# A recurrence chain next to an expert layer: running two neighbouring items half an item apart

## The chip, the cores and the metric

One core of a Trainium2 chip runs the whole program. The metric is the device time of one execution in microseconds (us), lower is better: 1274.45 us is the median of 3 runs of the kernel before (1274.09 to 1287.01).

## The reference, cut

Three layers follow each other. The first is a linear recurrence over 768 steps for 4 x 8 heads, each with a 40 x 40 state:

```python
for t in range(S):
    y[:, :, t] = np.einsum('bhd,bhde->bhe', rt, state)
    Sa = np.einsum('bhde,bhe->bhd', state, at)
    state_decay = state * wt[:, :, None, :] - np.einsum('bhd,bhe->bhde', Sa, bt)
    state = state_decay + np.einsum('bhd,bhe->bhde', vt, kt)
```

Its output goes through a dense layer (`h = x @ w_in`, `g = max(0.01*h, h)`, `g @ w_out`, 3072 tokens of 320, hidden 2048), and that through eight experts with top-1 routing (`relu(x @ w1[e]) @ w2[e]`, scaled by the gate).

## The kernel before, in words

Time is cut into chunks of 64 steps, and the recurrence within a chunk is solved with matrix products. An **item** is one chunk for eight heads; there are 48. Items alternate between two states, `S[0]` for even and `S[1]` for odd numbers, so item i needs the state that item i-2 left and nothing of item i-1. The Tile scheduler sets the order on each engine from the order of the code and priorities; every engine then works in that order and holds at an instruction whose input is not there.

For the work on an item i this text uses one letter for each group of TensorE matmuls, with the lines of the kernel before:

- **T** (L551): four transposes of loaded columns; DVE multiplies them to `KB` (L553).
- **P** (L559, L564): the two masked products; ACT copies them out (L570), POOL masks them (L572).
- **S** (L591): state times right sides, into the PSUM tile `y`; ACT copies (L595).
- **R** (L601): right-hand sides of the triangular system; ACT copies to `X` (L602).
- **V** (L607): inverse times right-hand sides; DVE (L612) and ACT (L614) write the result, with its sign turned, into `F`.
- **z** (L622): the state's update, which DVE adds to the state (L624). **y** (L628): the outputs; DVE scales them to `Y` (L631) and SP stores them (L636).
- Items 6, 7, 14, 15, 30, 31, 38 and 39 also turn the state back (L643).

T and P of item i+1 belong to the generator `late(i+1)`, which is stepped beside `chain(i)`: T before S of item i, P right behind V of item i. The loads for item j (`late_load(j)`, L530 to L540, all issued by SP) stand in the code behind item j-3.

Two other streams fill TensorE between these groups. `moe` is the dense layer: L686 (first product, 8 matmuls of 256 columns a piece) and L707 (second product, 6 of 328 columns a piece). `early` prepares the triangular inverses for eight items at a time: products on L463, a long run of DVE work (L475 to L501), and two small products for each of four chunks (L507, L515). `run` mixes the streams with `merge`, which takes steps in proportion to given weights: per item five steps of the chain, ten of `early` and eight of `moe`.

PSUM banks are handed out by `s.banks`: bank 0 to `early`, bank 1 to T and P (`sl`), bank 2 to `y` (`cy`), bank 3 to R, V, z and the turns (`cx`), 4 to 7 to `moe`. So one bank holds `y` of every item from 4 on.

Behind item 47 the rest of `moe` runs, and then the experts (phase 2, L1073 to L1146), which the change leaves alone.

Of the kernel before, what the change touches and what calls it, by code (L numbers as in the profile page):

```python
# [16 lines left out]
ALU = mybir.AluOpType  # L17
# [7 lines left out]
RST = 4  # L25
NFC = FF // 128
# [7 lines left out]
HC = 75  # L34
FB = 7
HI = 5
# [13 lines left out]
P0 = 5  # L50
P1 = 5
# [4 lines left out]
def bc(ap, shape):  # L56
    return ap.to_broadcast(shape)
# [73 lines left out]
class Phase1:  # L131
    def __init__(s, tc, es, I, out, x1d, chip):
        s.tc, s.nc, s.es, s.I, s.out, s.x1d, s.chip, s.lg = tc, tc.nc, es, I, out, x1d, chip, chip.lg
        nc = s.nc
        g = nc.gpsimd
        s.ident = chip.ident
        bank = lambda *k: Ring([chip.bank[n] for n in k])
        s.banks = {"se": bank(0), "sl": bank(1), "cy": bank(2), "cx": bank(3), "m1": bank(4, 5), "m2": bank(6, 7),
                   "cy1": bank(6), "cx1": bank(7)}
        s.dp = es.enter_context(tc.tile_pool(name="dp", bufs=1, space=DRAM))  # L140
        s.right = chip.room("p1", "right")
        A = s.right.new
# [34 lines left out]
        for h in range(2):  # L177
            m = s.nmask[64 * h:64 * h + 64, :]
# [71 lines left out]
    def decide(s):  # L250
        nc, v = s.nc, s.nc.vector
        v.reduce_max(s.lim[:, 0:1], s.chip.flags, axis=mybir.AxisListType.X)
        pt = s.psum("se")[0:1, 0:128]
# [164 lines left out]

    def early(s, e):
        nc = s.nc  # L420
        ps = lambda: s.psum("m1") if e == 0 else s.psum("se")
# [4 lines left out]
        for c4 in range(4):  # L426
# [33 lines left out]
            for p in range(8):  # L460
                for pi in range(2):
                    q = 64 * (1 - pi)
# [79 lines left out]
    def late(s, i):  # L542
# [4 lines left out]
        la = lL[:, 512:1024].rearrange("q (k p t) -> q k p t", k=2, t=64)  # L547
        nc.sync.dma_start(W[q104], s.dW[i // 2][:, p4])
        pw = s.psum("sl")
# [4 lines left out]
        yield  # L554
        ps = s.psum("sl").rearrange("q (p t) -> q p t", t=128)
# [10 lines left out]
        yield  # L566
        for pi in range(2):
            r = 64 * pi
            Fv = F[r:r + 64, :, pi, 0:128]
            nc.scalar.copy(Fv, ps[r:r + 64])  # L570
            Fv = Fv.rearrange("q p (a t) -> q p a t", a=2)
            nc.gpsimd.affine_select(out=Fv, in_=Fv, compare_op=ALU.is_gt, fill=0.0, base=0,  # L572
                                    pattern=[[0, 4], [0, 2], [1, 64]], channel_multiplier=-1)
        yield


    def chain(s, i, beside=iter(())):
        nc = s.nc
        hh, C, gg = i // 24, (i // 2) % 12, i % 2
        F, RI, W, KB = s.slot(i)  # L580
        S, X, Y = s.S[gg], s.X[i % 2], s.Y[i % 2]
        e = hh * 3 + C // 4
        Inv = s.Inv[e % 2][:, C % 4, 4 * gg:4 * gg + 4]
        v = lambda t: t[:, 0:416].rearrange("q (p t) -> q p t", t=104)
        if C == 0 and hh == 1:
            nc.vector.memset(S, 0.0)
        cy, cx = ("cy", "cx") if i > 3 or i % 2 == 0 else ("cy1", "cx1")
        y = v(s.psum(cy))
        for p in range(4):
            for q in (64, 0):  # L590
                nc.tensor.matmul(y[q:q + 40, p, :], lhsT=S[q:q + 40, p, :], rhs=RI[q:q + 40, p, :],  # L591
                                 start=(p == 0), stop=False, skip_group_check=True)
        for pi in range(2):
            q = 64 * (1 - pi)
            nc.scalar.copy(F[q:q + 40, :, pi, 64:168], y[q:q + 40])  # L595
        yield
        x = v(s.psum(cx))
# [4 lines left out]
        nc.scalar.copy(X, x)  # L602
        yield
        x = v(s.psum(cx))
# [10 lines left out]
        for _ in beside:  # L615
            pass
        yield
        z = s.psum(cx)[:, 0:160].rearrange("q (p t) -> q p t", t=40)
        for p in range(4):
            for pi in range(2):  # L620
                q = 64 * (1 - pi)
                nc.tensor.matmul(z[q:q + 40, p, :], lhsT=F[:, p, pi, 128:168], rhs=KB[:, p, 1 - pi, :], start=True, stop=True)  # L622
        for q in (64, 0):
            nc.vector.tensor_tensor(S[q:q + 40], S[q:q + 40], z[q:q + 40], op=ALU.add)  # L624
        for p in range(4):
            for pi in range(2):
                q = 64 * (1 - pi)
                nc.tensor.matmul(y[q:q + 40, p, 0:64], lhsT=KB[:, p, 1 - pi, :], rhs=F[:, p, pi, 64:128],  # L628
                                 start=False, stop=True, skip_group_check=True)
# [8 lines left out]
        if C % RST == RST - 1 and C < 11:  # L638
            def turn(x):
                t = s.psum("cx")[:, 0:160].rearrange("q (p t) -> q p t", t=40)  # L640
                for p in range(4):
                    for q in (64, 0):
                        nc.tensor.matmul(t[q:q + 40, p, :], lhsT=x[q:q + 40, p, :], rhs=s.ident[q:q + 40, q:q + 40],  # L643
                                         start=True, stop=True)
                return t
            t = turn(S)
            for q in (64, 0):
                nc.vector.tensor_tensor(s.ST[q:q + 40], t[q:q + 40], bc(W[q:q + 40, :, 64:65], [40, 4, 40]), op=ALU.mult)
            t = turn(s.ST)
            for q in (64, 0):  # L650
                nc.scalar.copy(S[q:q + 40], t[q:q + 40])
            yield


    def moe_load(s, v):
# [74 lines left out]
    def run(s, p2):  # L730
# [68 lines left out]
        for i in range(48):  # L799
# [21 lines left out]
            next(beside, None)  # L821
# [615 lines left out]
```

## Time and profile before

| | |
|---|---|
| median of 3 runs | 1274.45 us |
| profiled execution, its own time | 1275.27 us |
| span of that execution (first to last instruction) | 1273.6 us |
| mean granted TensorE clock | 0.942 |
| PE (TensorE matmuls) busy | 1037.1 us, 81% |
| DVE busy | 800.0 us, 63% |
| ACT busy | 511.8 us, 40% |
| POOL busy | 408.0 us, 32% |

PE is the engine that is busiest, yet busy shares are a mean over very different stages; what counts is which wait ends last in a stage. "Granted clock" is the share of full speed that TensorE was given; it takes the values 1.0 (2.4 GHz) and 0.5 (1.2 GHz), and a mean between them says how the time was divided.

How the rows further down read. A stretch: its bounds and length in us, then busy us and number of instructions of PE, PEld (weight loads), DVE, ACT and POOL, the granted clock, the DMA share and GB/s. A timeline: start, duration, engine (SPq is SP's queue), line, operation, output<-inputs, shapes, count, and in brackets the idle time before it and what ended it; instructions of a line that follow each other are merged. Waits: who waited for whom, us in total, times, the longest. Groups by line: busy us, mean ns of one, idle time before them and what ended it.

### The profile page before, as it was taken

Reading aid. Unit: us, or ns where it says so; the run is one execution under the profiler, and the core shown is the slowest. Engines: PE = TensorE matmul, PEld = TensorE weight load, DVE = VectorE, ACT = ScalarE, POOL = GpSimd, SP = SyncE. Lnnn points to the kernel's source line nnn. Section 1 sums busy time; section 2 is a strip of 40 time slices with the busy share of each in tenths; the row PEclk is TensorE's granted clock in tenths of the full one; section 3 lists DMA queues with packets and bytes.
Section 4 is the critical chain, followed back from the end, with each engine's and each line's share of the span. In section 5 each row is a group of like instructions: output and inputs, shape, how many; then the busy total and the mean of one; then the engine's idle time right before and its main releaser. Section 6 shows DMA issues by size and latency. Waiting matters only on the chain. (4 is left out here: it accounts for less than half of the span.)

```text
span 1273.6 us, 31259 instructions
## 1 busy us (share of the span) xinstructions
PE 1037.1 (81%) x12429; PEld 937.0 (74%) x12429; DVE 800.0 (63%) x1677; ACT 511.8 (40%) x1113; POOL 408.0 (32%) x458
## 2 busy tenths in 40 slices
PE   1348943599889989898979988999998968979994
PEld 1336732478778878787878878889898958878983
DVE  4698597894696558855884579544368445543541
ACT  1334442345435354455434543444443235332330
POOL 3364453444321332234222332122242321432210
PEclk9999999999998989998987989999999988989998
DMA  6665265347534654466434644233233444533100
GB/s 166 155 169 138 76 170 153 110 100 181 147 93 101 151 148 104 108 163 162 104 102 105 166 118 113 71 96 91 73 110 103 132 125 126 183 104 106 32 21 20
DMA packets 215735, 149.52 MB, mean 117 GB/s; under 512 B 152820, under 2 KB 195979, under 8 KB 213061
## 3 DMA queue, kind: packets, MB, share of 16 engines
q1 hardware_dynamic: 211949, 138.47, 41.7%
q0 software_dynamic: 3504, 7.75, 2.0%
q8 instruction: 122, 2.00, 0.7%
q14 instruction: 160, 1.31, 0.4%
HBM read 112.39 MB, written 37.21 MB: 117 GB/s over the span
## 5 line engine op out<-in xcount | busy, mean ns | idle before, releaser
L707 PE MATMUL bank<-w,m 128*128 128x328 f32 x792 | 151.2, 329 | 1.6 <-ACT m L691 1.3
L1123 PE MATMUL bank<-p,p 128*128 128x256 f32 (+1 forms) x704 | 121.5, 332 | 33.3 <-issue 26.9
L1123 PEld LDWEIGHTS bank<-p,p 128*128 128x128 f32 x704 | 113.8, 208 | 37.8 <-issue 30.0
L686 PE MATMUL bank<-m,w 128*128 128x256 f32 x768 | 125.0, 309 | 7.2 <-DVE m L690 7.1
L707 PEld LDWEIGHTS bank<-w,m 128*128 128x128 f32 x792 | 122.2, 193 | 9.7 <-issue 2.5
L690 DVE TENSOR_TENSOR m<-bank,m 128x512 f32<-128x512 f32 x96 | 66.8, 696 | 87.5 <-ACT m L689 87.0
L686 PEld LDWEIGHTS bank<-m,w 128*128 128x128 f32 x768 | 106.5, 205 | 14.8 <-DVE m L690 7.6
L686 PE MATMUL bank<-g,w 128*128 128x256 f32 x768 | 114.9, 298 | 0.0
L693 POOL TENSOR_TENSOR m<-m,m 128x128 fp32r<-128x128 f32 x66 | 46.1, 699 | 192.1 <-ACT m L691 185.0
L686 PEld LDWEIGHTS bank<-g,w 128*128 128x128 f32 x768 | 101.4, 198 | 5.5 <-issue 2.0
L572 POOL TENSOR_SCALAR_AFFINE_SELECT p<-p 64x512 f32<-64x512 f32 x94 | 67.3, 716 | 104.4 <-ACT p L570 102.5
L689 ACT ACTIVATE m<-bank 128x512 f32<-128x512 f32 x96 | 57.2, 596 | 96.9 <-PE bank L686 66.7
L1140 PE MATMUL bank<-p,p 128*128 128x320 f32 x600 | 93.3, 311 | 0.0
L1140 PEld LDWEIGHTS bank<-p,p 128*128 128x128 f32 x600 | 88.5, 188 | 0.0
L463 PE MATMUL bank<-p 40*64 40x64 f32 x736 | 35.7, 262 | 57.0 <-POOL p L453 22.2
L485 DVE TENSOR_TENSOR p<-p 128x30 f32<-128x30 f32 (+9 forms) x180 | 74.1, 412 | 3.5
L463 PEld LDWEIGHTS bank<-p 40*64 40x64 f32 x736 | 32.1, 172 | 60.1 <-issue 25.6
L1146 POOL DMA_INDIRECT out<-p,p x25 | 25.0, 999 | 156.5 <-DVE p L1145 114.9
L483 DVE TENSOR_TENSOR p<-p 128x30 f32<-128x30 f32 (+9 forms) x180 | 69.5, 386 | 3.2
L707 PE MATMUL bank<-w,g 128*128 128x328 f32 x360 | 70.2, 340 | 0.0
L612 DVE TENSOR_TENSOR p<-bank,p 64x256 f32<-64x256 f32 x94 | 39.6, 421 | 46.5 <-PE bank L607 30.6
L1126 ACT ACTIVATE p<-bank 128x384 fp32r<-128x384 f32 (+2 forms) x88 | 36.3, 415 | 78.3 <-PE bank L1123 66.0
(234 smaller groups left out, 2199.4 us busy)
## 6 DMA issues: line engine op xcount, KB each, us to landing
p<-in_e_wabk SPq DMA_DIRECT2D x22, 835.7 KB
p<-in_w SPq DMA_DIRECT2D x8, 1280.0 KB
p<-di SPq DMA_DIRECT2D x96, 104.0 KB
p<-in_w SPq DMA_DIRECT2D x8, 1024.0 KB
p<-in_t_kb SPq DMA_DIRECT2D x48, 160.0 KB
dw<-p SPq DMA_DIRECT2D x24, 211.2 KB
di<-p SPq DMA_DIRECT2D x24, 208.0 KB
p<-dk SPq DMA_DIRECT2D x48, 104.0 KB
```

The costliest lines, as they stand in the source:

```text
L463: m3 = nc.tensor.matmul(pB[q:q + 64, p, :], lhsT=eb[q:q + 40, p, :], rhs=ea[q:q + 40, p, :], start=True, stop=True)
L483: nc.vector.tensor_tensor(tm, bc(P[:, j + 1:32, j:j + 1], [128, n, j]), bc(P[:, j:j + 1, 0:j], [128, n, j]), op=ALU.mult)
L485: s.step = nc.vector.tensor_tensor(P[:, j + 1:32, 0:j], P[:, j + 1:32, 0:j], tm, op=ALU.add)
L572: nc.gpsimd.affine_select(out=Fv, in_=Fv, compare_op=ALU.is_gt, fill=0.0, base=0, pattern=[[0, 4], [0, 2], [1, 64]], channel_multiplier=-1)
L612: nc.vector.tensor_tensor(F[q:q + 64, :, pi, 64:128], x[q:q + 64, :, 0:64], bc(s.nmask[q:q + 64, None, :], [64, 4, 64]), op=ALU.mult)
L686: nc.tensor.matmul(o, lhsT=l, rhs=r, start=(n == 0), stop=(n == 7))
L689: nc.scalar.mul(g, ph, 0.01)
L690: nc.vector.tensor_tensor(g, ph, g, op=ALU.max)
L693: nc.gpsimd.tensor_tensor(gL[:, GS:512], g[:, GS:512], gH[:, GS:512], op=ALU.subtract)
L707: nc.tensor.matmul(po[tt], lhsT=l[:, ts], rhs=r[:, fc, :], start=(fc == 0 and n == 0), stop=(fc == NFC - 1 and n == 2))
L1123: nc.tensor.matmul(o, lhsT=l, rhs=r, start=(i == 0), stop=(i == 7))
L1140: nc.tensor.matmul(po, lhsT=l[:, ts], rhs=r[:, fc, :], start=(fc == 0 and i == 0), stop=(fc == 7 and i == 2))
```

## The change

The chain's generator is cut into pieces, and from item 4 on `chained(i)` runs two neighbouring items half an item apart. One run on TensorE holds V of item i and S of item i+1 (with P of item i+2 between or behind), the next run y and z of item i and R of item i+1; T of item i+2 closes the item. So P moves from item i-1 to item i-2, a whole item earlier against its own item, while the place of `late_load` stays. An item has two chain steps and one for T where it had five, so its weight in `merge` is 3.

The banks change: `y` gets two (`ya`, bank 2, and `yb`, bank 1, by odd and even), z goes into columns 64 to 104 of the same `y` bank, and T, P and all of `early` share bank 0. Inside y and z the order turns: y first, then z. The matmuls, copies and loads of an item are otherwise the same in number and size. Before item 4, `late(5)` and the first half of item 4 run as an opening; `prep` loses bank 0 for its transposes.

```diff
-        s.banks = {"se": bank(0), "sl": bank(1), "cy": bank(2), "cx": bank(3), "m1": bank(4, 5), "m2": bank(6, 7),
+        s.banks = {"s": bank(0), "ya": bank(2), "yb": bank(1), "cx": bank(3), "m1": bank(4, 5), "m2": bank(6, 7),
                    "cy1": bank(6), "cx1": bank(7)}
...
+    def outputs(s, i):
+        nc = s.nc
+        F, RI, W, KB = s.slot(i)
+        y = s.y[i]
         for p in range(4):
             for pi in range(2):
                 q = 64 * (1 - pi)
-                nc.tensor.matmul(z[q:q + 40, p, :], lhsT=F[:, p, pi, 128:168], rhs=KB[:, p, 1 - pi, :], start=True, stop=True)
+                m = nc.tensor.matmul(y[q:q + 40, p, 0:64], lhsT=KB[:, p, 1 - pi, :], rhs=F[:, p, pi, 64:128],
+                                     start=False, stop=True, skip_group_check=True)
+        with s.tc.issue_after(m.ins):
+            for p in range(4):
+                for pi in range(2):
+                    q = 64 * (1 - pi)
+                    nc.tensor.matmul(y[q:q + 40, p, 64:104], lhsT=F[:, p, pi, 128:168], rhs=KB[:, p, 1 - pi, :],
+                                     start=True, stop=True, skip_group_check=True)
...
+    def chained(s, i):
+        n, j = i + 1 < 48, i + 2 < 48
+        x = s.solve(i)
+        if j:
+            ps = s.late_products(i + 2)
+        if n:
+            s.state(i + 1)
+        s.solve_out(i, x)
+        if n:
+            s.state_out(i + 1)
+        if j:
+            s.late_masks(i + 2, ps)
+        yield
+        s.outputs(i)
+        if n:
+            x = s.rhs(i + 1)
+        s.outputs_out(i)
+        if n:
+            s.rhs_out(i + 1, x)
+        yield
+        if s.turns(i):
+            s.turn(i)
+            yield
+        if j:
+            s.late_kb(i + 2)
+        yield
...
-            wo = s.wout_chunks(wT, wg, Ring([s.chip.bank[n] for n in (0, 4, 5)]), range(P0 + P1, NFC))
+            wo = s.wout_chunks(wT, wg, Ring([s.chip.bank[n] for n in (4, 5)]), range(P0 + P1, NFC))
...
-            beside = s.late(i + 1) if 3 < i < 47 else iter(())
-            next(beside, None)
-            gens = [(ahead(s.tc, s.chain(i, beside), HC, HC) if i < HI else s.chain(i, beside), 5 + (1 if (i // 2) % 12 % RST == RST - 1 else 0))]
+            if i == 4:
+                for g in (s.late(5), s.opening(4)):
+                    for _ in ahead(s.tc, g, HC, HC):
+                        pass
+            c = s.chain(i) if i < 4 else s.chained(i)
+            gens = [(ahead(s.tc, c, HC, HC) if i < HI else c, (5 if i < 4 else 3) + s.turns(i))]
```

The order of TensorE (PE) in the steady stretch, before: from z and y of item 41 to S of item 43. `bank_61` to `bank_64` are banks 0 to 3; each "..." leaves out matmuls of `moe` alone, in turn 12, 16, 8, 16, 14 and 6 of them.

```order
L622 MATMUL bank_64<-p_112,p_110 40x40 x8
L628 MATMUL bank_63<-p_110,p_112 40x64 x8
...
L551 MATMUL bank_62<-all_72,p_102 128x104 x4
L591 MATMUL bank_63<-p_103,p_115 40x104 x8
...
L601 MATMUL bank_64<-p_108 64x104 x8
...
L607 MATMUL bank_64<-p_117,p_99 64x104 x8
L559 MATMUL bank_62<-p_104,p_102 64x64 x8
L564 MATMUL bank_62<-p_109,p_102 64x64 x8
...
L622 MATMUL bank_64<-p_111,p_108 40x40 x8
L628 MATMUL bank_63<-p_108,p_111 40x64 x8
...
L551 MATMUL bank_62<-all_72,p_101 128x104 x4
...
L591 MATMUL bank_63<-p_104,p_116 40x104 x8
```

The same place on PE with the change, from V of item 41 to V of item 42. L639 is V, L565 and L570 P (of item 43), L610 S (of item 42), L659 y, L665 z, L626 R, L552 T; the "..." leave out 18, 12 and 14 matmuls of `moe`.

```order
L639 MATMUL bank_64<-p_118,p_99 64x104 x8
L565 MATMUL bank_61<-p_104,p_102 64x64 x8
L570 MATMUL bank_61<-p_109,p_102 64x64 x8
L610 MATMUL bank_63<-p_103,p_115 40x104 x8
...
L659 MATMUL bank_62<-p_110,p_112 40x64 x8
L665 MATMUL bank_62<-p_112,p_110 40x40 x8
L626 MATMUL bank_64<-p_108 64x104 x8
...
L552 MATMUL bank_61<-all_72,p_102 128x104 x4
...
L639 MATMUL bank_64<-p_117,p_99 64x104 x8
```

Four chain runs an item became two, and each step of the chain has more `moe` matmuls between it and what feeds it.

The second place is P of item 28 on PE. Before, it stands right behind V of item 27; the "..." leaves out 14 matmuls of `moe`.

```order
L607 MATMUL bank_64<-p_118,p_99 64x104 x8
L559 MATMUL bank_62<-p_104,p_101 64x64 x8
L564 MATMUL bank_62<-p_109,p_101 64x64 x8
...
L622 MATMUL bank_64<-p_112,p_108 40x40 x8
```

With the change it stands by itself behind R of item 27 and ahead of V of item 27; the "..." leave out 21, 9 and 2 matmuls of `moe`.

```order
L626 MATMUL bank_64<-p_108 64x104 x8
...
L565 MATMUL bank_61<-p_104,p_101 64x64 x8
L570 MATMUL bank_61<-p_109,p_101 64x64 x8
...
L552 MATMUL bank_61<-all_72,p_101 128x104 x4
...
L639 MATMUL bank_64<-p_118,p_99 64x104 x8
```

The scheduler did not place it in the run of item 26 as the code has it, but one run later; of the 38 items from 10 on it set P apart like this for 12 (11 to 15, 20, 22, 28, 30, 36, 37 and 40), and T of item 28 follows P on the same bank.

## Rows read from the trace of the kernel before

**Rows 1.** Busy time of each engine and granted clock in two stretches.

```profile
298.38:842.50 544.12, 493.08 (x7243) 438.03 (x7242) 372.23 (x770) 247.90 (x533) 161.34 (x184) 0.92 0.50 124
842.50:917.46 74.96, 74.96 (x1022) 68.23 (x1021) 31.64 (x67) 35.02 (x69) 20.30 (x25) 1.00 0.35 88
```

**Rows 2.** PE timeline: S of items 8, 40 and 46 begins.

```profile
298.38 0.73 PE L591 MATMUL bank<-p,p 40*40 40x104 f32 x12
...
842.50 0.91 PE L591 MATMUL bank<-p,p 40*40 40x104 f32 x16
...
917.46 0.91 PE L591 MATMUL bank<-p,p 40*40 40x104 f32 x16
```

**Rows 3.** Who PE waited for, 298.38 to 842.50 us.

```profile
PE bank L463 <- POOL p L453: 13.6, 8, 3.1
PE bank L591 <- DVE p L631: 12.5, 8, 2.8
PE bank L628 <- DVE p L612: 9.2, 6, 3.8
PE bank L607 <- ACT p L602: 4.9, 2, 3.2
PE bank L622 <- ACT p L614: 3.6, 5, 0.9
PE bank L507 <- ACT p L518: 2.1, 5, 1.0
PE bank L601 <- ACT p L595: 1.8, 1, 1.8
```

**Rows 4.** PE timeline: one and two pieces of `moe` between chain runs.

```profile
858.93 1.17 PE L707 MATMUL bank<-w,m 128*128 128x328 f32 x6
860.03 0.66 PE L607 MATMUL bank<-p,p 64*64 64x104 f32 x10
...
861.53 2.08 PE L707 MATMUL bank<-w,g 128*128 128x328 f32 x12
863.53 0.51 PE L622 MATMUL bank<-p,p 128*40 128x40 f32 x16
```

**Rows 5.** Busy time and granted clock around five long waits.

```profile
378.00:392.00 14.00, 11.59 (x99) 9.85 (x99) 9.90 (x29) 3.33 (x7) 3.09 (x2) 0.63 0.38 99
...
456.00:470.00 14.00, 11.52 (x142) 10.38 (x142) 5.90 (x13) 5.78 (x14) 5.13 (x6) 0.65 0.76 191
...
586.00:597.00 11.00, 7.80 (x114) 7.08 (x112) 5.39 (x12) 4.71 (x11) 4.80 (x5) 0.69 0.81 220
655.00:683.00 28.00, 24.23 (x322) 21.14 (x322) 13.52 (x19) 9.75 (x23) 3.16 (x5) 0.57 0.35 86
788.00:798.00 10.00, 7.53 (x53) 6.60 (x51) 8.08 (x25) 2.73 (x5) 2.57 (x3) 0.67 0.30 71
```

**Rows 6.** Timeline of DVE, then of PE, around the wait at 656 us.

```profile
657.41 1.93 DVE L498 STREAM_TRANSPOSE p<-p 128x1024 f32<-128x1024 f32 x1
...
659.86 0.44 PE L628 MATMUL bank<-p,p 128*40 128x64 f32 x2 [3.77 <-DVE p L612]
```

**Rows 7.** Timelines of SP and PE: loads and what follows, three places.

```profile
212.19 0.88 SPq L530 DMA_DIRECT2D p<-di  x2
...
216.24 0.93 PE L551 MATMUL bank<-all,p 104*128 104x104 f32 x4 [5.92 <-DMA p<-di]
...
338.14 0.66 PE L607 MATMUL bank<-p,p 64*64 64x104 f32 x10
...
345.24 0.87 SPq L536 DMA_DIRECT2D p<-in_l_r  x1
...
609.37 0.87 SPq L536 DMA_DIRECT2D p<-in_l_r  x1
...
610.93 0.30 PE L607 MATMUL bank<-p,p 64*64 64x104 f32 x1
```

**Rows 8.** Groups by line, ACT, 298.38 to 842.50 us: copies of P.

```profile
L570 ACT COPY p<-bank 64x512 f32<-64x512 f32 x64 | 37.1, 580 | 10.0 <-PE bank L564 8.8
```

More of the change, by code (lines that the diff above doesn't have):

```diff
@@ L540, in late_load, with late_kb @@
         nc.sync.dma_start(tok, s.I["t_kb"][i])
-    def late(s, i):
+    def late_kb(s, i):
         nc = s.nc
@@ L565, in late, with late_masks @@
                                  start=True, stop=True)
-        yield
+        return ps
+    def late_masks(s, i, ps):
+        nc = s.nc
+        F = s.slot(i)[0]
         for pi in range(2):
@@ L573, in late, with tiles, state @@
                                     pattern=[[0, 4], [0, 2], [1, 64]], channel_multiplier=-1)
+    def late(s, i):
+        s.late_kb(i)
         yield
-    def chain(s, i, beside=iter(())):
+        ps = s.late_products(i)
+        s.late_masks(i, ps)
+        yield
+    def tiles(s, i):
+        hh, C, gg = i // 24, (i // 2) % 12, i % 2
+        other = i in (1, 3)
+        return hh, C, gg, s.S[gg], s.X[i % 2], ("cy1" if other else "yb" if i % 2 else "ya"), "cx1" if other else "cx"
+    v104 = staticmethod(lambda t: t[:, 0:416].rearrange("q (p t) -> q p t", t=104))
+    def state(s, i):
         nc = s.nc
-        hh, C, gg = i // 24, (i // 2) % 12, i % 2
+        hh, C, gg, S, X, cy, cx = s.tiles(i)
         F, RI, W, KB = s.slot(i)
[L581 to L584, printed above, removed]
         if C == 0 and hh == 1:
             nc.vector.memset(S, 0.0)
-        cy, cx = ("cy", "cx") if i > 3 or i % 2 == 0 else ("cy1", "cx1")
-        y = v(s.psum(cy))
+        y = s.y[i] = s.v104(s.psum(cy))
         for p in range(4):
@@ L592, in chain, with state_out, rhs @@
                                  start=(p == 0), stop=False, skip_group_check=True)
+    def state_out(s, i):
+        F, y = s.slot(i)[0], s.y[i]
         for pi in range(2):
             q = 64 * (1 - pi)
-            nc.scalar.copy(F[q:q + 40, :, pi, 64:168], y[q:q + 40])
-        yield
-        x = v(s.psum(cx))
+            s.nc.scalar.copy(F[q:q + 40, :, pi, 64:168], y[q:q + 40])
+    def rhs(s, i):
+        nc = s.nc
+        F, cx = s.slot(i)[0], s.tiles(i)[-1]
+        x = s.v104(s.psum(cx))
         for p in range(4):
@@ L601, in chain, with rhs_out, solve @@
                 nc.tensor.matmul(x[q:q + 64, p, :], lhsT=F[:, p, pi, 0:64], rhs=F[:, p, pi, 64:168], start=True, stop=True)
-        nc.scalar.copy(X, x)
-        yield
-        x = v(s.psum(cx))
+        return x
+    def rhs_out(s, i, x):
+        s.nc.scalar.copy(s.X[i % 2], x)
+    def solve(s, i):
+        nc = s.nc
+        hh, C, gg, S, X, cy, cx = s.tiles(i)
+        Inv = s.Inv[(hh * 3 + C // 4) % 2][:, C % 4, 4 * gg:4 * gg + 4]
+        x = s.v104(s.psum(cx))
         for p in range(4):
@@ L614, in chain @@
             nc.scalar.mul(F[q:q + 64, :, pi, 128:168], x[q:q + 64, :, 64:104], -1.0)
[L615 to L618, printed above, removed]
+    def outputs(s, i):
+        nc = s.nc
+        F, RI, W, KB = s.slot(i)
+        y = s.y[i]
         for p in range(4):
@@ L621, in chain, with outputs_out @@
                 q = 64 * (1 - pi)
-                nc.tensor.matmul(z[q:q + 40, p, :], lhsT=F[:, p, pi, 128:168], rhs=KB[:, p, 1 - pi, :], start=True, stop=True)
-        for q in (64, 0):
[L624 to L629, printed above, removed]
+                m = nc.tensor.matmul(y[q:q + 40, p, 0:64], lhsT=KB[:, p, 1 - pi, :], rhs=F[:, p, pi, 64:128],
[6 more added lines that the diff above has]
+                                     start=True, stop=True, skip_group_check=True)
+    def outputs_out(s, i):
+        nc = s.nc
+        hh, C, gg, S, X, cy, cx = s.tiles(i)
+        W, Y, y = s.slot(i)[2], s.Y[i % 2], s.y.pop(i)
+        for q in (64, 0):
+            nc.vector.tensor_tensor(S[q:q + 40], S[q:q + 40], y[q:q + 40, :, 64:104], op=ALU.add)
         for q in (64, 0):
@@ L636, in chain, with turns @@
             nc.sync.dma_start(xv[pi, gg, C % 2], Y[q:q + 40])
-        yield
[L638 to L651, printed above, removed]
-            yield
+    def turns(s, i):
+        C = (i // 2) % 12
+        return C % RST == RST - 1 and C < 11
@@ new lines, in turn, with go @@
+    def turn(s, i):
+        nc = s.nc
+        S, cx, W = s.S[i % 2], s.tiles(i)[-1], s.slot(i)[2]
+        def go(x):
+            t = s.psum(cx)[:, 0:160].rearrange("q (p t) -> q p t", t=40)
+            for p in range(4):
+                for q in (64, 0):
+                    nc.tensor.matmul(t[q:q + 40, p, :], lhsT=x[q:q + 40, p, :], rhs=s.ident[q:q + 40, q:q + 40],
+                                     start=True, stop=True)
+            return t
+        t = go(S)
+        for q in (64, 0):
+            nc.vector.tensor_tensor(s.ST[q:q + 40], t[q:q + 40], bc(W[q:q + 40, :, 64:65], [40, 4, 40]), op=ALU.mult)
+        t = go(s.ST)
+        for q in (64, 0):
+            nc.scalar.copy(S[q:q + 40], t[q:q + 40])
@@ new lines, in chain, with opening @@
+    def chain(s, i):
+        s.state(i)
+        s.state_out(i)
+        yield
+        s.rhs_out(i, s.rhs(i))
+        yield
+        s.solve_out(i, s.solve(i))
+        yield
[4 more added lines that the diff above has]
+            s.turn(i)
+            yield
+    def opening(s, i):
+        s.state(i)
+        s.state_out(i)
+        yield
+        s.rhs_out(i, s.rhs(i))
+        yield
+    def chained(s, i):
[10 more added lines that the diff above has]
+            s.late_masks(i + 2, ps)
+        yield
+        s.outputs(i)
+        if n:
+            x = s.rhs(i + 1)
+        s.outputs_out(i)
+        if n:
+            s.rhs_out(i + 1, x)
+        yield
+        if s.turns(i):
+            s.turn(i)
+            yield
+        if j:
+            s.late_kb(i + 2)
+        yield
```

19 lines of the change are left out of this document (12 added, 7 removed).

## The prediction

> **What bounds the kernel now.** I read the page's slices first, then busy times by stretch, then who PE waited for, then single places on the timeline. PE is dense almost everywhere, so the question is what still takes time from it. The answer comes from comparing two stretches of the chain. From S of item 40 to S of item 46 no inverse is prepared and PE never idles: 74.96 us for six items, 12.5 us an item at full clock [rows 1, 2]. From S of item 8 to S of item 40 the same step takes 544.12 / 32 = 17.0 us [rows 1, 2]. The difference is 4.5 us an item, 144 us in all. Three parts can be told:
>
> - PE waits. The list for this stretch sums to 50.7 us; its seven largest entries are shown [rows 3].
> - The clock. A mean of 0.92 over 544.12 us means 2 x 0.08 x 544 = 87 us at 1.2 GHz [rows 1]. It falls behind the waits: five places hold 10.4 + 9.8 + 6.8 + 24.1 + 6.6 = 58 us of it, each as 2 x (1 - clock) x length [rows 5]; two of them begin behind S, two behind V, the long one behind y.
> - The rest, some 50 us, is work: the matmuls of `early` and the turns.
>
> So a gain of this change can only be PE's lost time in the chain, about 50 us of waits and some 35 us of clock (87 us x 0.81 busy / 2; the busy share is 62.7 of 77 us in [rows 5]), and what it costs PE to go in and out of chain runs. DVE, busy for 372 of 544 us there, is no bound over the stretch [rows 1], but it comes late in bursts.
>
> **1. Runs of the chain.** Six L707 matmuls between R and V take 860.03 - 858.93 = 1.10 us from start to start; twelve between V with P and z take 863.53 - 861.53 = 2.00 us [rows 4]. The second six thus cost 0.90 us, and breaking the stream once costs 0.20 us. An item had four runs apart from T; it now has two, and a third for the 12 of 38 items whose P was set apart (the order of the change). That saves 40 items x 2 x 0.20 - 12 x 0.20 = 13.6 us; I take 13.
>
> **2. Waits that go.** By the order, the distance between a step and what feeds it is now 18 to 24 `moe` matmuls behind V and S, and 26 plus T behind R, where R to V had 8.
>
> - S waiting for DVE's scaling of the outputs (12.5 us, at most 2.8) [rows 3]: this is no data, since S of item i+1 uses the other state. It is the one `y` bank, which DVE still reads. Two banks put the reader a whole item back: 12.5 us go. What S needs next is the state that DVE added to, one run and some 26 matmuls earlier (0.12 to 0.15 us each, rows as in [rows 4], so over 3 us, plus R): the 2.8 us are covered.
> - V waiting for the copy to `X` (4.9 us, two waits, at most 3.2) [rows 3]: from 8 matmuls to 26 and T, 2 us or more further away. Gone, or 1 us left; I count 4.9.
> - R waiting for the state's copies (1.8 us, and 1.2 us listed as issue): 3.0 go, as P, 18 matmuls, y and z now stand between.
> - z waiting for ACT (3.6 us, at most 0.9) [rows 3]: covered by y, which now goes first, and by S: 3.6 go.
> - y waiting for DVE (9.2 us, six times, at most 3.8) [rows 3]: the distance grows by S alone, and the long one, 3.77 us, is DVE at transposes of 1.93 us, which L612 stood behind [rows 6]. I take 5.2 of 9.2.
> - L463 waiting for POOL (13.6 us) and the small waits of `early` stay: nothing of them moves on purpose.
>
> Together 12.5 + 4.9 + 3.0 + 3.6 + 5.2 = 29 us.
>
> **3. A wait that comes.** P of item j now stands in the code in the first run of item j-2, and the loads it reads are issued behind item j-3. TensorE takes its matmuls in order, so a P that waits holds V, S and `moe`. How long a load takes: L530 is issued at 212.19 us and releases T at 216.24 us, 4.05 us [rows 7]. Where SP's queue is free a load issued behind item j-3 has about one item, 12.5 us, and lands in time. Not so behind the stores of `early` in SP's queue: for item 28 it is issued at 609.37 us and V of item 26 begins at 610.93; for item 12 it is issued at 345.24 us, and V of item 10 began at 338.14 us [rows 7]. There P right behind V would wait 345.24 + 4.05 - (338.14 + 0.5) = 10.7 us, and at item 28 2.0 us. The same subtraction for all items gives nine waits (items 12 to 14, 20, 21, 28, 29, 36, 37), 25 us; the first and item 28 are the two shown. That is one bound. The other is nothing, since the order set P back at most of these places (to behind R, 28 of those, as shown). I take 6 us, nearer to nothing, mostly item 12.
>
> *What a page says.* The Trainium skill, "DMA: Bandwidth & Descriptors", section "Anatomy of one DMA", gives about 2.0 us of fixed cost for a transfer on POOL's path; no row here shows so quick a release of PE by a load. By it the bound of 25 would be about 11 us and the term 3 instead of 6, a sum of 1221 us.
>
> **4. The clock.** With the waits go the falls behind them: the four shorter places of [rows 5] (33.6 us at half clock) and half of the long one (12), which starts with a y wait that only shrinks. Against that, two new falls behind P's waits, 8 us. 38 us at half clock, busy for 0.81 of it, give back 38 x 0.81 / 2 = 15 us.
>
> **5. At no cost.** The second half of `y`'s bank for z, the turned order of y and z (0.5 us later for DVE's add, with over 3 us to S), ACT's copies in another order (its copies, 1.0 us for two, have P, 18 matmuls, y and z ahead of R): hidden by the distances of part 2, and worth those waits again if a distance falls under 2 us. `prep` with two banks instead of three: DVE sets the pace there. The opening costs one item's first half ahead of the mix; below nothing too, items 4 to 7 may gain, 0 to 10 us.
>
> Sum: 13 + 29 - 6 + 15 = 51 us. From the profiled execution's own 1275.27 us this gives **1224 us**; the median of the runs is 0.8 us lower, which changes nothing here. What `moe` and the experts have behind the chain begins as much earlier, and nothing of it waits for a clock of its own.
>
> **Rivals.**
>
> - **The loads eat the gain.** P stands where it waits, near the 25 us bound, and the nine waits also pull the clock down at nine places: 13 + 29 - 25 + about 4 of clock = 21 us, 1254 us. For it: SP's queue is as late as [rows 7] shows and the chain now wants data an item earlier. Against: the order set those P back.
> - **The waits only move.** The bursts on DVE and POOL decide, and a chain that asks earlier waits as long; only runs are saved, 1262 us. For it: y's wait in [rows 6] and 13.6 us of L463. Against: four of the seven waits in [rows 3] are shorter than the distance added.
> - **One bank for T, P and `early`: slower.** Place: bank 0, where a writer must wait for the reader of the one before it. In the 32 items that is 64 groups of T and P and 48 of `early`, 112 hand-overs. P's reader is two ACT copies of 0.58 us, 1.16 us [rows 8], plus what ACT has queued. If every hand-over waited so, 130 us; it turns the sign from 51 / 112 = 0.46 us each, and is slower by 1% from 0.57 us. At 0.8 us, 90 us: 1313 us. Against: the order puts matmuls between (11 between P and T of item 28, over 1.2 us). The Trainium skill, "PSUM — Partial Sum Buffer", section "Summary: rules for kernel authors", asks for just the opposite of this edit: a matmul beside a read should go to another bank. No row of before shows bank 0 shared in this way.
> - **More than I count.** No wait for loads, y's wait gone, items 4 to 7 gain: about 1203 us.
>
> **How the numbers follow.** Forecast (1210 to 1240) 0.55; more 0.08; loads 0.19; only moved 0.10; one bank 0.08. The range takes in the forecast, most of "more" and of "loads": 1202 to 1260 us; some 0.2 is left out, mainly above. What a measurement of this kernel can tell from no change is about 1%, 12.7 us. Faster by over 1% (under 1261.7): 0.55 + 0.08 + 0.15 = 0.78; within 1%: 0.13; slower: 0.09.
>
> **What would show it.** After the change an item without `early` (40 to 46) should take 12.1 us instead of 12.5: that is part 1 alone. In the list of PE's waits the entries S for DVE, V for ACT and z for ACT should be near nothing, L463 for POOL about as large, and a new entry P for a DMA small. The mean clock from item 8 to 40 should be 0.95 or more. I am wrong if P waits at every round of `early`, if T, P or L507 wait for ACT or DVE at bank 0, or if the clock stays at 0.92 although the waits went.

## The result, and the profile after

| | before | with the change |
|---|---|---|
| median of 20 runs each | 1280.46 us (1272.27 to 1289.82) | 1299.56 us (1284.71 to 1315.6) |
| ratio, 95% interval | | 1.0113 (1.0078 to 1.0148) |
| profiled execution, own time | 1275.27 us | 1284.71 us |
| mean granted TensorE clock | 0.942 | 0.896 |
| PE busy | 1037.1 us | 1027.6 us |

The forecast was 1224 us (1202 to 1260) and faster. It came out 1.1% slower, some 14 us. The ratio leaves disturbed runs out, so it is not the quotient of the two medians; the profiled execution after is the shortest of its 20.

The stretches of the kernel after, as in [rows 1] (S of item 8 begins at 280.10 us, of item 40 at 850.20, of item 46 at 922.52):

```profile
0.00:280.10 280.10, 153.31 (x1733) 126.57 (x1734) 205.49 (x464) 100.60 (x255) 124.70 (x137) 0.81 0.55 143
```

```profile
280.10:850.20 570.10, 499.04 (x7470) 451.32 (x7470) 385.87 (x793) 250.82 (x546) 169.23 (x188) 0.90 0.48 119
850.20:922.52 72.32, 72.32 (x1073) 68.35 (x1071) 33.42 (x71) 35.69 (x72) 21.30 (x26) 1.00 0.38 95
```

S of item 8 comes 18 us earlier than before, but with less done: 325 fewer matmuls lie ahead of it, up to there PE is busy 16.8 us less and DVE 19.3 us less, and that work is done later. Part of it stands in the middle row, which is therefore not quite like for like: 570 us where before had 544, with 227 more matmuls, 192 of them the inverse's small products (L508 and L516, busy 33.4 us for 25.4). Of the 26 us more, 6 are busy time of PE (499.04 for 493.08), at a clock of 0.90 for 0.92, and 20 are waits. Who PE waited for there, to be held against [rows 3]:

```profile
PE bank L464 <- POOL p L454: 19.3, 8, 5.2
PE bank L508 <- DVE p L554: 15.6, 4, 4.9
PE bank L695 <- DVE p L700: 5.6, 2, 2.9
PE bank L659 <- DVE p L647: 4.8, 4, 1.5
PE bank L552 <- ACT p L580: 3.5, 3, 1.5
PE bank L464 <- POOL p L582: 3.3, 1, 3.3
PE bank L565 <- DVE p L554: 3.3, 3, 1.6
PE bank L565 <- DMA p<-in_l_r: 2.5, 2, 1.4
...
PE bank L464 <- ACT p L580: 1.5, 1, 1.5
PE bank L610 <- DVE p L675: 1.4, 1, 1.4
...
PE bank L626 <- ACT p L617: 0.9, 3, 0.4
...
PE bank L639 <- ACT p L630: 0.2, 1, 0.2
```

The whole list sums to 70.8 us; before it was 50.7. The chain's own waits did what was forecast: y (L659) 4.8, S (L610) 1.4, R (L626) 0.9, V (L639) 0.2 and z none, 7.3 us for the 33 us before. The rest together grew from 17.5 to 63.5 us. The products of the inverse (L464) wait 24.1 us in three entries, where L463 had 13.6 (the one put down to POOL's L582 ends, on the timeline, with ACT's copy of P, L580, at 612.93 us: L464 begins at 613.03); L508 has a new wait of 15.6 us, T and P wait for each other's readers at bank 0, and the turn (L695) waits 5.6 us.

One of the four waits of L508, on PE and then on DVE. T of the item (L552) has just been written to bank 0, and L508 writes the same bank:

```profile
540.10 0.52 PE L552 MATMUL bank<-all,p 104*128 104x104 f32 x4
...
545.56 0.76 PE L508 MATMUL bank<-p,p 32*32 32x32 f32 x32 [4.21 <-DVE p L554]
```

```profile
535.23 2.06 DVE L496 STREAM_TRANSPOSE p<-p 128x1024 f32<-128x1024 f32 x1
...
539.03 3.90 DVE L502 STREAM_TRANSPOSE p<-p 32x1024 f32<-32x1024 f32 x2
542.95 0.65 DVE L673 TENSOR_TENSOR p<-p,bank 40x160 f32<-40x160 f32 x2
...
544.43 0.67 DVE L792 TENSOR_TENSOR m<-bank,m 128x512 f32<-128x512 f32 x1
545.03 0.47 DVE L554 TENSOR_TENSOR p<-bank,p 128x320 f32<-128x320 f32 x1
```

The data that L508 multiplies come from L496 and were there at 537.3 us. It is the reader of T (L554) that comes late, behind three more transposes (L499 and the two of L502) and everything that piled up behind them. The other three waits look the same: in all four a transpose of L502 ends 0.2 to 2.1 us ahead of L554.

### The profile page after: what moved, and what is told of

The parts are those of the page before. It is cut to its first block, busy times and chain, and to the rows that moved or that the text cites. A ratio compares the mean times of both kernels' runs of the same rounds, so it can differ in the third digit from the quotient of the medians.

```text
span 1282.9 us, 31097 instructions
## 1 busy us (share of the span) xinstructions
PE 1027.6 (80%) x12429; PEld 939.3 (73%) x12429; DVE 796.6 (62%) x1677; ACT 510.5 (40%) x1113; POOL 409.4 (32%) x458
## 5 line engine op out<-in xcount | busy, mean ns | idle before, releaser
L809 PE MATMUL bank<-w,m 128*128 128x328 f32 x792 | 148.6, 329 | 2.3 <-DVE m L794 1.7
L788 PE MATMUL bank<-m,w 128*128 128x256 f32 x768 | 126.0, 312 | 7.2 <-DVE m L792 6.9
L788 PEld LDWEIGHTS bank<-m,w 128*128 128x128 f32 x768 | 108.9, 209 | 13.4 <-DVE m L792 7.5
L792 DVE TENSOR_TENSOR m<-bank,m 128x512 f32<-128x512 f32 x96 | 65.8, 685 | 84.8 <-ACT m L791 84.5
L788 PE MATMUL bank<-g,w 128*128 128x256 f32 x768 | 109.8, 292 | 0.0
L788 PEld LDWEIGHTS bank<-g,w 128*128 128x128 f32 x768 | 99.1, 194 | 4.6 <-issue 2.4
L582 POOL TENSOR_SCALAR_AFFINE_SELECT p<-p 64x512 f32<-64x512 f32 x94 | 70.1, 745 | 98.9 <-ACT p L580 91.0
L464 PE MATMUL bank<-p 40*64 40x64 f32 x736 | 35.7, 262 | 70.3 <-POOL p L454 23.9
L464 PEld LDWEIGHTS bank<-p 40*64 40x64 f32 x736 | 31.6, 171 | 75.5 <-issue 27.9
L809 PE MATMUL bank<-w,g 128*128 128x328 f32 x360 | 67.6, 330 | 1.7 <-ACT g L793 1.2
L793 ACT CAST m<-m 128x512 fp32r<-128x512 f32 x66 | 40.8, 618 | 70.8 <-DVE m L792 70.3
```

The source lines that it names most:

```text
L464: m3 = nc.tensor.matmul(pB[q:q + 64, p, :], lhsT=eb[q:q + 40, p, :], rhs=ea[q:q + 40, p, :], start=True, stop=True)
L788: nc.tensor.matmul(o, lhsT=l, rhs=r, start=(n == 0), stop=(n == 7))
L792: nc.vector.tensor_tensor(g, ph, g, op=ALU.max)
L793: nc.scalar.copy(gH, g)
L809: nc.tensor.matmul(po[tt], lhsT=l[:, ts], rhs=r[:, fc, :], start=(fc == 0 and n == 0), stop=(fc == NFC - 1 and n == 2))
```

## The experiments

Ratios are to the kernel before, timed on the same chip beside each; "items 8 to 40" is the stretch from S of item 8 to S of item 40 as in [rows 1]. The changed kernel was timed once, as in the table above (1.0113, 1.0078 to 1.0148), so a difference to it is one between two ratios, each with its interval; below some 0.7% it can't be told from noise.

**The shared bank in the old order.**

```
-        pw = s.psum("sl")
+        pw = s.psum("se" if i > 7 else "sl")
-        ps = s.psum("sl").rearrange(...)
+        ps = s.psum("se" if i > 7 else "sl").rearrange(...)
```

> The kernel before, with one edit: from item 8 on T and P use bank 0, which `early` uses too; bank 1 stays empty. Theory A (the shared bank): in the changed kernel PE waited 27 us in items 8 to 40 where a user of bank 0 follows another one's late reader, 15.6 us of it L508 for DVE's KB product of T. If that is the cause, it shows here without the new order of the chain: PE's list gets L507 <- DVE L553 with some 10 to 16 us and entries of T or P for ACT, the mean clock falls below 0.94, and the time is 20 to 40 us longer than before. Theory B (the order of the chain: asking half an item earlier is what makes PE wait, and the bank only gets the blame, since the inverse would wait for DVE's transposes anyway): within 6 us of before.

0.9964 (0.9921 to 1.0007). Theory A is wrong for the old order: the bank costs nothing there. In its list L507 waits 0.2 us, and the entries in which one user of that bank waits for another's reader are 1.7 us (L515 for DVE's L553) and 1.6 us (L463 for ACT's L570).

**The second `y` bank in the old order.** As above, and

```
+        cy = "yb" if i > 7 and i % 2 else cy
```

> The kernel before in its old order, but with the banks of the change from item 8 on: T, P and `early` on bank 0, `y` on banks 2 and 1 in turn. Against the run with the shared bank alone this shows what the second y bank is worth: the 12.5 us that S waited for DVE's scaling should go, and some clock with them, 12 to 20 us less than that run. Theory A: still 5 to 25 us slower than before, since the price of bank 0 stays. Theory B: 12 to 20 us faster than before. What is left between this run and the changed kernel is the order of the chain alone.

0.9984 (0.9951 to 1.0018). Both theories miss, and this is the sharpest result of the study. The run with the shared bank alone has in its list

```profile
PE bank L628 <- DVE p L612: 12.9, 7, 2.5
PE bank L591 <- DVE p L631: 10.8, 10, 2.5
PE bank L622 <- ACT p L614: 10.6, 7, 3.8
PE bank L463 <- POOL p L453: 9.9, 6, 4.3
```

and with the second bank (the lines are one further down)

```profile
PE bank L629 <- DVE p L613: 13.1, 7, 2.5
PE bank L623 <- ACT p L615: 11.8, 7, 3.9
PE bank L463 <- POOL p L453: 11.6, 7, 5.6
PE bank L608 <- ACT p L603: 3.3, 2, 2.1
PE bank L602 <- issue: 2.5, 6, 1.3
```

S's wait of 10.8 us is gone entirely, and yet the sum of the list is 50.6 us for 52.4. It did not pass to the next step that needs DVE: y's wait for DVE grew by 0.2 us, while the entries that name ACT, POOL or no releaser ("issue") grew from 26.4 to 36.1 us. Which of the engines holds the others is not shown by this run.

This run has the banks of the changed kernel from item 8 on, in the old order of the chain. The changed kernel is 1.3% longer than it (1.0113 against 0.9984, the intervals apart). So what costs is the new order with what else came with it, not the banks alone.

**T off bank 0 in the new order.**

```
-        pw = s.psum("s")
+        pw = s.psum("m1" if i > 5 else "s")
```

> The changed kernel with one edit: from item 6 on T goes to the two banks of moe's first product (4 and 5, in turn) instead of bank 0. Theory A: L508 <- DVE L554 (15.6 us) and P <- DVE L554 (3.3 us) go, and the half clock behind them (65 us of the 109 us in items 8 to 40 begin at the four L508 waits); 25 to 40 us faster than the changed kernel, so 0.98 to 0.99 of before. A price may come up in moe, whose first product then waits for DVE at that bank: up to 10 us. Theory B: no more than 6 us from the changed kernel, with the waits under another name.

1.0031 (0.9993 to 1.0070), 10 us less than the changed kernel and still not faster than before. L508 <- DVE L554 is gone, but L788 waits 11.7 us and T 5.0 us for DVE's L792 instead, and the list sums to 58.0 us for 70.8.

**T and P apart from `early`, with moe on one bank in both.** The first pair of lines is in both runs (`m1x` is bank 4 alone), the second in the test only, for T and likewise for P (`lt` is bank 5):

```
-            ph = s.psum("m1")
+            ph = s.psum("m1x")
...
-        pw = s.psum("s")
+        pw = s.psum("lt" if i > 7 else "s")
```

> The control for the next run: the changed kernel with moe's first product on one bank (4) instead of two; T, P and `early` still share bank 0, and bank 5 is empty behind the opening. It is slower than the changed kernel by what moe loses with one bank: both theories say 5 to 30 us, with new waits of L788 for DVE and ACT.

> As the run before (moe's first product on bank 4 alone), but T and P on bank 5 from item 8 on, so that `early` has bank 0 to itself: the only difference between the two is the shared bank, in the new order of the chain. Theory A (bank 0 is what the new order waits for: L508 <- DVE L554, P <- DVE L554, T <- ACT's copies of P, L464 <- the copies of P, 27 us together): those five entries are gone and the time is 15 to 40 us less than in the control. Theory B (the waits belong to DVE's and ACT's bursts and only change their name): the entries go, others take their place, and the time is within 6 us of the control.

1.0179 (1.0104 to 1.0255) and 1.0079 (1.0047 to 1.0111): the bank is worth 1.0%, some 13 us, a little under what A wanted; the two intervals just touch, and the control has four runs. But not by fewer waits. In the test

```profile
PE bank L464 <- POOL p L454: 22.9, 9, 5.0
...
PE bank L508 <- DVE p L496: 5.7, 2, 4.2
PE bank L508 <- ACT p L519: 5.3, 2, 4.9
```

L508, which in the control waited 10.5 us for L554 and 2.8 us for L496, now waits 11.0 us for the inverse's own transposes and copies; the lists sum to 62.2 and 67.0 us. What differs is the clock, 0.89 and 0.91, and PE's busy time, 509.07 and 494.13 us; why the clock differs is not shown.

**P and T one item later.** P: `s.late_products(i + 1)` and its masks in the first run of item i instead of `i + 2`. T: `s.late_kb(i + 1)` between `s.outputs(i)` and `s.rhs(i + 1)` instead of `s.late_kb(i + 2)` at the end.

> The changed kernel with P moved back: the first run of item i holds P of item i+1, as before the change, instead of P of item i+2. The entries of P for a DMA (3.5 us in items 8 to 40) go. P's masks now stand closer to R of item i+1, so R may wait for POOL or ACT. Theory A: bank 0 stays shared, so L508 <- DVE L554 stays near 15 us; the time is 0 to 8 us less than the changed kernel. Theory C (that the loads, with the queues of ACT and POOL that stand behind a late P, start the chain of waits): 15 us or more less, with L464 <- POOL back at some 13 us.

1.0095 (1.0060 to 1.0130): the loads ahead of P are not the cause, and theory C falls; L464 <- POOL stays at 18.6 us.

> The changed kernel with T moved back by most of an item: T of item i+2 stands between z and R of item i+1 instead of at the end of item i. Bank 0 stays shared, but T no longer stands alone behind R, and an item has one break of moe's stream less (0.2 us, 8 us in all). Theory A: what counts is whether T's reader on DVE is late when `early` wants the bank; DVE's KB product now stands in DVE's queue near the state's update, and the wait of L508 for L554 shrinks from 15.6 us to under 6: 10 to 25 us less than the changed kernel. Theory B: only the 8 us of the breaks, with L508 waiting as long for another instruction of DVE or ACT.

1.0042 (0.9997 to 1.0088), some 9 us less, with intervals that overlap: no more than what the saved break of moe's stream gives (B).

**The inverse's products later.** One number, the empty steps of `early` between POOL's work and L464:

```
-PD = 2
+PD = 5
```

> The changed kernel with one number changed: `early` takes five empty steps (PD) instead of two between POOL's multiplication and its products on PE (L464), so PE comes to L464 some 0.3 of an item later; a round of `early` then needs 79 of its 80 steps. Theory B (PE is now ahead of the chain of one inverse: load, DVE's scans, POOL's L454; what the new order takes off PE's way only brings it earlier to these waits): L464 <- POOL falls from 19.3 us to under 8, the half clock from 109 us to under 80, and the time by 15 to 30 us. Theory A (bank 0 is what costs): under 8 us, and L508 <- DVE L554 stays.

> The control: the same five empty steps in the kernel before. Theory B: its L464 waits (13.6 us) go too, for less: 0 to 12 us faster, unless the waits of y, S and V for DVE take them over (then 0). Theory A says nothing on it.

0.9822 (0.9747 to 0.9896) and, in the old order, 0.9948 (0.9910 to 0.9987). The number alone takes 2.9%, 37 us, off the changed kernel, more than B had said; the median of its four runs is 1263.98 us, below both kernels. (The two profiled executions differ by 20 us, 1264.84 for 1284.71, and the latter is the shortest of its 20.) L464 <- POOL L454 is 0.2 us there. The list sums to 54.2 us for 70.8 and now begins

```profile
PE bank L552 <- ACT p L466: 13.4, 4, 4.9
PE bank L508 <- DVE p L554: 6.7, 3, 3.9
```

Two more values of the number, four also with three empty steps ahead of L508, and five with T moved:

> The changed kernel with four empty steps ahead of L464 and nothing else. If the distance decides: 20 to 32 us less than the changed kernel (0.987 to 0.996), and the three steps ahead of L508 in the run with both undid most of it, by moving L508 onto the next item's y (19.2 us of y <- DVE there). If the time is near the run with both (1.00), four steps are too few or the order is a matter of single places.

> The changed kernel with two more empty steps ahead of L464 and, in rounds 2 to 5 of `early`, three between DVE's last transposition and L508. Theory B: both sorts of waits of the inverse (L464 <- POOL 19.3 us, L508 <- DVE L554 15.6 us, which had DVE's transposes ahead of it) shrink by more than half, and the half clock behind them too: 25 to 45 us less than the changed kernel, so below the kernel before. Theory A: as the run with L464 alone, since bank 0 is still shared.

> The changed kernel with no empty step ahead of L464 instead of two. If PE's arrival at L464 ahead of POOL is what sets the time: L464 <- POOL grows from 19.3 us to 30 us or more, and the time by 10 to 30 us, to 1.02 to 1.035 of before. If the gain of five steps came from some other shift of the order: within 8 us of the changed kernel, either way.

> The changed kernel with T one item later (as in the run with that alone, some 9 us faster) and five empty steps ahead of L464. If the two causes are apart the gains add: 25 to 40 us less than the changed kernel, 0.98 to 0.99 of before. If both only move the same waits, no more than the better of the two alone.

Four steps: 1.0046 (1.0013 to 1.0078); four and three ahead of L508: 1.0009 (0.9979 to 1.0039); no step: 1.0049 (1.0013 to 1.0085); five with T later: 0.9866 (0.9771 to 0.9961), no better than five alone. So the time does not follow the distance, against the first expectation for four steps and for none. L464's wait does (25.1 us with no step, 19.3 with two, 6.6 with four, 0.2 with five), but others come: with four steps

```profile
PE bank L659 <- DVE p L647: 33.1, 17, 4.0
PE bank L464 <- POOL p L454: 6.6, 2, 4.1
```

y waits 33.1 us where it waited 4.8. What is late there, on SP's queue, PE and DVE of the run with four steps:

```profile
576.93 0.56 SPq L416 DMA_DIRECT2D p<-in_e_wabk  x1
```

```profile
581.00 0.66 PE L639 MATMUL bank<-p,p 64*64 64x104 f32 x10
...
589.99 0.31 PE L659 MATMUL bank<-p,p 128*40 128x64 f32 x2 [3.95 <-DVE p L647]
```

```profile
585.23 0.43 DVE L243 TENSOR_SCALAR p<-p 104x512 f32<-104x512 f32 x1 [5.59 <-DMA p<-in_e_wabk]
...
589.51 0.43 DVE L647 TENSOR_TENSOR p<-bank,p 64x256 f32<-64x256 f32 x1
```

V of the item ends by 582 us and DVE stands idle, yet V's product (L647) runs at 589.5: ahead of it in DVE's queue is L243, the first instruction on a chunk that `early` loads. It starts 8.3 us after the issue of the load (576.93 to 585.23), and the scans behind it and one instruction of `moe` take another 4 us of DVE before L647. y waits for both.

**T off bank 0 once L464 is later.** Five steps and T on moe's banks; then P later as well.

> The changed kernel with five empty steps ahead of L464 and T on moe's banks 4 and 5. If bank 0 costs by itself: T <- ACT L466 (13.4 us) and L508 <- DVE L554 (6.7 us) of the run with five steps alone go, and the time is 8 to 20 us less than in that run: 0.966 to 0.976 of before. If the waits only change their name: within 6 us of that run (0.978 to 0.987), with L788 or T waiting for DVE instead.

> As the run before, and P one item later as it was before the change. P then has its loads in time (its waits for DMA, 3 us in the run with five steps, go) but stands closer to R. If P an item early is a price: 3 to 8 us less than the run before; if not, the same or up to 8 us more, with R <- POOL.

0.9904 (0.9864 to 0.9945) and 0.9827 (0.9729 to 0.9924). Neither beats five steps alone (0.9822), and the intervals of the two overlap, so P's place is worth nothing that shows here either. Of the two expectations for the first, that the waits only change their name is the nearer: L788 now waits 20.2 us for L792 and 6.3 us for L554, and the list sums to 60.3 us.

**The part that DVE waits for, loaded first.** In `early_load`, both orders:

```
-            s.nc.sync.dma_start(t, src)
+            for c in ((0, 521), (521, 2057)) if e > 1 else ((0, 2057),):
+                s.nc.sync.dma_start(t[:, c[0]:c[1]], src[:, c[0]:c[1]])
```

> The changed kernel, with the load of a chunk of `early` (rounds 2 to 5) cut in two transfers: first the 521 columns that DVE's L243 and the scans read, then the other 1536. Theory R (DVE holds at L243 for the load, and the chain's own DVE work stands behind it in the queue): DVE's wait at L243 for the load falls from 26.9 us to under 14, L464 <- POOL from 19.3 us to under 13, and the time by 8 to 20 us. Rival: the transfer is late because it is issued late, or the scans only come earlier and wait for something else: L243's wait stays over 20 us, or the time stays within 6 us of the changed kernel.

> The same edit in the kernel before, where DVE waited 20.1 us at this instruction. Theory R: 0 to 10 us faster than before, less than in the changed kernel, since the old order left more of the waits to the chain's own banks (y's bank 12.5 us), which this does not touch. Rival: within 6 us.

0.9973 (0.9929 to 1.0016), which is 1.4% less than the changed kernel, and 0.9878 (0.9789 to 0.9968, four runs) in the old order. The kernel before took 1289.84 us beside these two, where it took 1278 to 1283 us beside the other runs, so the ratios may flatter them; by the medians themselves each edit takes 12 to 13 us off (1287.16 for 1299.56, 1267.91 for 1280.46). DVE's wait for the load in items 8 to 40, in the order before, after, after with the edit, before with the edit (L242 and L243 are the same instruction):

```profile
DVE p L242 <- DMA p<-in_e_wabk: 20.1, 10, 4.7
```

```profile
DVE p L243 <- DMA p<-in_e_wabk: 26.9, 11, 5.1
```

```profile
DVE p L243 <- DMA p<-in_e_wabk: 13.1, 10, 2.9
```

```profile
DVE p L242 <- DMA p<-in_e_wabk: 10.7, 6, 5.4
```

About half of this wait of DVE is gone, and 12 to 18 us of either kernel's time. PE's list falls from 70.8 to 61.3 us and from 50.7 to 45.6. Items 8 to 40 hold as many matmuls as without the edit, give or take one, and take 9.9 us less in the new order (560.18 for 570.10) and 11.8 us less in the old one (532.34 for 544.12):

```profile
285.46:845.64 560.18, 498.65 (x7471) 451.30 (x7472) 390.55 (x793) 250.77 (x546) 164.43 (x188) 0.90 0.48 121
```

```profile
296.26:828.60 532.34, 486.12 (x7243) 431.25 (x7243) 366.12 (x764) 248.36 (x535) 164.17 (x184) 0.94 0.50 126
```

Theory R holds in place and size for the new order. Whether the old order gains less, as expected, is not settled: its ratio leaves 0.3 to 2.1%. Nor is this wait all there is: with four steps DVE waits 40.9 us at L243, 14 us more than in the changed kernel, and the time is not longer.

The two orders side by side, each pair with the same edit:

| | old order | new order | new to old |
|---|---|---|---|
| as given | 1 | 1.0113 | +1.1% |
| five steps ahead of L464 | 0.9948 | 0.9822 | -1.3% |
| decay loaded first | 0.9878 | 0.9973 | +1.0%, intervals overlap |

The order of the chain has no price of its own here: with two steps ahead of L464 the new one is the longer, with five the shorter. One number that places the inverse's products turns the sign; at which places of the order it does so is not shown.

## Why the prediction was wrong, by its steps

- **Part 1, runs of the chain: right.** Items 40 to 46 take 72.32 / 6 = 12.05 us for the 12.49 before; 12.1 was forecast. Where nothing is prepared beside it, the new order gives its 0.44 us an item. (The work in the two stretches is not quite the same: 192 and 144 of moe's matmuls for 169 and 156, and 32 of a turn; so 0.44 is a size, not an exact price.)
- **Part 2, waits that go: the entries right, the sum wrong.** The five entries fell from 33 to 7.3 us, 26 for the 29 counted. But 20 us more are waited in all: entries other than these went from 17.5 to 63.5 us. This is the step that failed. It took each entry as a price of the pair that it names, and asked only whether that pair moved apart. S <- L631 had DVE late behind the inverse's work, as in its longest wait before, where two transposes (L478) stand ahead of the scaling (lines of DVE and PE below); and the second bank alone (0.9984 against 0.9964) shows that nothing is won when S alone stops waiting. "L463 waiting for POOL (13.6 us) and the small waits of `early` stay: nothing of them moves on purpose" was the visible half of it, a growth put at nothing: 13.6 us became 19.3, with 4.8 more at the bank, and L508 came to 16.5, where L507 had 2.1. That PE comes to these waits sooner when the chain no longer holds it is argued; with five steps ahead of L464 its wait for L454 is 0.2 us.

```profile
347.12 3.96 DVE L478 STREAM_TRANSPOSE p<-p 32x1024 f32<-32x1024 f32 x2
...
352.27 0.42 DVE L631 TENSOR_TENSOR p<-bank,p 40x256 f32<-40x256 f32 x1
```

```profile
352.74 0.91 PE L591 MATMUL bank<-p,p 40*40 40x104 f32 x16 [2.78 <-DVE p L631]
```

- **Part 3, loads: right in size.** P <- DMA is 3.5 us for the 6 counted, and moving P back gains nothing that can be measured.
- **Part 4, the clock: wrong in sign,** since it hung on part 2. At 0.90 over 570.1 us it is 114 us at 1.2 GHz for 87: 27 x 0.81 / 2 = 11 us lost, an estimate, where 15 were to be given back. Waits (20) and clock (11) less the runs (13) make 18 us; with the 8 us of the inverse's small products that stand in items 8 to 40 now, and stood ahead of item 8 before, that is the 26 us by which the stretch is longer. Of the 18, 9 us were seen between the two profiled executions and 14 by the ratio; the difference of 4 to 9 us is not told apart.
- **Part 5.** Items 4 to 7 did not gain: S of item 8 begins 18 us earlier with 325 matmuls, 16.8 us of PE's busy time, not yet done.
- **The rivals.** "The waits only move" had the mechanism and too small a price: it let the chain's waits come back at their own size, and not that the inverse's would grow past them. "One bank" was nearest in sign. Its entries sum to 27 us (L508 15.6, T and P 6.8, L464 4.8), 0.24 us for each of 112 hand-overs, where 0.46 had to be passed. The rule of the Trainium skill, "PSUM — Partial Sum Buffer", section "Summary: rules for kernel authors", that a matmul beside a read goes to another bank, is borne out here only in part: in the old order sharing costs nothing (0.9964), in the new one 1.0% (intervals that just touch), and with L464 later taking T off the bank gains nothing.

**Shown:** taking one of PE's waits away does not shorten the kernel by it (the second bank: 50.6 us in all for 52.4), since others grow, often for another instruction of DVE (T off bank 0; four steps). And shortening one wait of DVE, for the load of a chunk, gives 12 to 18 us in both orders. The trace of the changed kernel has this load ahead of the three longest waits of L464 (5.2, 4.1 and 3.6 us): DVE holds at L243 for it (2.0, 5.1 and 2.5 us), then come the scans (L449), then POOL's L454 (in the first of the three behind two masks of L582), then L464. The third of them, on DVE, POOL and PE:

```profile
741.47 0.43 DVE L243 TENSOR_SCALAR p<-p 104x512 f32<-104x512 f32 x1 [2.51 <-DMA p<-in_e_wabk]
```

```profile
746.86 1.17 POOL L454 TENSOR_TENSOR p<-p,p 104x512 f32<-104x512 f32 x1 [2.04 <-DVE p L449]
```

```profile
748.25 1.02 PE L464 MATMUL bank<-p 40*64 40x64 f32 x14 [3.60 <-POOL p L454]
```

The four waits of L508 are of another kind: DVE holds for no load in the 9 us ahead of them, but works through four of the inverse's own transposes (L496, L499, twice L502). **Argued only:** that one lateness is behind all the waits, the smaller ones too, and that the new order made them longer by bringing PE to them sooner. **Open:** why five steps give 37 us and four 9, and why no step is not slower than two although its waits sum to as much (69.7 us). The scheduler deals the whole order anew for each edit, so single places may decide, and a run with the order held and one instruction moved was not made. Nor was the mixture of five steps with the load cut in two. Moving the inverse's small products (L508, L516) off bank 0 was tried, but that edit changes what the kernel computes, so its time (1.0177) stands for nothing.

## What to carry to other kernels

The entries of a list of waits may be one cost with several doors: closing a door moved the wait to another one here, not always of the same engine, so the sum of the list has to be forecast, not its entries. Look in the late engine's own queue for what it holds at (here a load), and shorten that; only then reorder the engine that waits. And before two streams share a PSUM bank, ask where the reader of each stands in its engine's queue, not how long it runs.

## What was not expected of the hardware

In the first 300 us the granted clock of the rows and the pace of the matmuls part ways. The row gives 0.81 over the first 280 us of the kernel after and 0.98 over the first 298 of before. The run with the shared bank in the old order, whose instructions differ from those of before from item 8 on alone, has 0.80; yet PE is busy as long in it, and S of item 8 begins at 298.05 us for 298.38. The two stretches, the run's and then before's:

```profile
0.00:298.06 298.06, 170.56 (x2056) 141.70 (x2056) 223.01 (x497) 107.35 (x274) 134.62 (x144) 0.80 0.53 139
```

```profile
0.00:298.38 298.38, 170.10 (x2058) 142.05 (x2059) 224.81 (x498) 108.00 (x276) 134.85 (x144) 0.98 0.53 138
```

From 160 to 230 us the clock stands at 0.50 in that run and at 1.00 in before. What a matmul of R took there (shortest, median and longest, in ns), in the run and in before, and then in before from S of item 40 to S of item 46, where the clock is 1.00 as well:

```profile
L601 PE MATMUL bank<-p x24: 377/381/436, 186.4 to 229.9; 128*64 128x104 f32 x24
```

```profile
L601 PE MATMUL bank<-p x16: 380/381/436, 190.1 to 191.9; 128*64 128x104 f32 x16
```

```profile
L601 PE MATMUL bank<-p x96: 252/253/303, 845.4 to 908.5; 128*64 128x104 f32 x96
```

At 0.50 and at 1.00 the same matmul took 381 ns there, half as long again as the 253 ns later on. So TensorE was as slow in before as in the other run, whatever the row says, and the lower figure cost nothing because nothing was slower. Behind item 8 the rows fit: from 655 to 683 us, at 0.57 in [rows 5], a matmul of R takes 381 ns (median) as well. A mean clock over a whole kernel therefore says little: 0.896 against 0.942 here is mostly the first stretch, and only the fall from 0.92 to 0.90 behind item 8 has a price.
